# Wider score products, unread TensorE products at the ends of the passes, and a shorter direct ending in a two-layer decode kernel

## The chip, the cores and the metric

The kernel runs on one core of one Trainium2 chip. The metric is the device time of one execution in microseconds (us). A core has TensorE (matrix products, written to PSUM), VectorE (DVE), ScalarE (ACT), GpSimd (POOL) and SyncE (SP), which here issues nearly all loads from device memory. A product of 32-bit floats is two instructions on TensorE in the trace, so a count in a trace row is twice the count in a row of the program's order.

## The reference

Two layers with the same weights, each an attention over a cache and a gated feed-forward block, for a batch of 2 and one new token each:

```python
# B, Sq, D = 2, 1, 448;  H, Sk, Dh = 16, 4096, 256;  F = 1792
def _A_ref(x, k_cache, v_cache, wq, wo):
    q = (x @ wq).reshape(B, Sq, H, Dh).transpose(0, 2, 1, 3)
    scores = jnp.einsum("bhqd,bhkd->bhqk", q, k_cache) * (Dh ** -0.5)
    p = _softmax(scores, axis=-1)
    o = jnp.einsum("bhqk,bhkd->bhqd", p, v_cache)
    return o.transpose(0, 2, 1, 3).reshape(B, Sq, H * Dh) @ wo

def _B_ref(x, W_gate, W_up, W_down):
    gate = x @ W_gate
    gate = gate * (gate > 0)
    return (gate * (x @ W_up)) @ W_down

x = x + _A_ref(_layernorm(x), k_cache, v_cache, wq, wo)
x = x + _B_ref(_layernorm(x), W_gate, W_up, W_down)
x = x + _A_ref(_layernorm(x), k_cache, v_cache, wq, wo)
x = x + _B_ref(_layernorm(x), W_gate, W_up, W_down)
```

Everything is float32. The caches do not fit on the chip, so each layer reads them from device memory: 561.5 MB over the run.

## The kernel before

A **unit** is one head of one batch element, 32 a layer. Its k and its v are 4 MB each, in four **chunks** of 1 MB. All loaded data lies in one SBUF tile, `arena`, cut into 27 places of 1 MB: six blocks of four, and three single ones. `pending` lists every load of the program in order; `pump` issues the next ones on SP (L127) as far as places are free, and `release` frees a place behind the last product that reads it and calls `pump`. Most k and v are loaded as whole blocks of 4 MB, the last twelve chunks of a pass one by one. The first layer goes through the units forward, the second backward; 22 chunks and one head's weights stay in the arena from the one to the other (`KEPT`). So while the first layer's feed-forward block runs, only four places are free for its eleven pieces of weights, and the later pieces, and the second layer's loads, wait until its products free more.

`attention` holds the loop over units that sets TensorE's order, since every engine works through its own list in program order:

- `score`: the products of q and one chunk of k. The scores of four groups of keys go to PSUM rows 0, 32, 64 and 96 of `raw`, 256 columns wide, two products for the two halves of the head dimension (L308). One copy a chunk by DVE to `found_s` (L314).
- `score_turn`: four products a chunk with the identity as right operand put the scores on the partitions (L321).
- `softmax_max`, `softmax_exp`: maximum (DVE, POOL), exponential and sum (ACT, POOL).
- `weigh`: probabilities times v, a chunk at a time, into four strips of 32 PSUM rows of `po` (L358), 512 columns wide.
- `out_copy`, `out_add` (ACT L369, DVE L372) collect the unit's result in `row`; `out_turn` (L380) and `out_keep` turn it, and `project` (L399) multiplies it by the output weights of the head, for every second unit, into `acc`. They come one unit later, behind the next unit's scores and softmax.
- `query` (L283, L286): q of the next head.

Behind the last unit `ffn` runs: `absorb` (L236, L238, L226, L228, L246) adds the attention's output to x and turns it; `proj` multiplies by the gate's half and then the up half of the first weights (L447, four strips, 448 columns, 32 in a row as two calls); L468 and L470 make the hidden vector; L474 and L476 turn it; L517 multiplies by the 14 chunks of the down weights in four strips (`pd`). In the second layer only the first seven chunks take that way and are summed into `y` by `add_rows` (L250); the other seven go straight to `y`, two rows of `acc` in the fourth strip (L522). `y` is copied by DVE and ACT (L540, L541) and written out by SP (L542).

Of the kernel before, what the change touches and what calls it, by code (L numbers as in the profile page):

```python
# [25 lines left out]
G, E = 4, 2  # L26
QN = E * P
# [39 lines left out]
def two_layers(  # L67
# [112 lines left out]
    found_s = consts.tile([P, 2, QN], F32, name="found_s")  # L180
# [30 lines left out]
    po_all = ps_o.tile([P, 2, 2 * DH], F32, name="po")  # L211
    nc.vector.memset(po_all, 0.0)

    raw = ps_r.tile([P, 2, 2 * DH], F32, name="raw")
    nc.vector.memset(raw, 0.0)
# [5 lines left out]
    y = acc[SUMS : SUMS + B]  # L221

# [44 lines left out]
    def attention(order, after, begun):  # L267
# [35 lines left out]
        def score(u, c):  # L303
            kt = get("k", order[u], c).rearrange("p (j g n) -> p j g n", j=2, g=G)
            half, at = c % 2, c // 2 * QN
            for j in range(2):
                for g in range(G):
                    nc.tensor.matmul(  # L308
                        raw[32 * g : 32 * g + 1, half, at : at + QN],
                        q_of[u][:, j, :], kt[:, j, g, :], start=(j == 0), stop=(j == 1),  # L310
                    )
# [4 lines left out]
        def score_turn(u, c):  # L316
            if c == 0:
                s_of[u] = ps_s.tile([P, NT], F32, name="small")
            for e in range(E):
                n = c * CT + e * G  # L320
                nc.tensor.matmul(  # L321
                    s_of[u][:, n : n + G], found_s[:, c % 2, e * P : (e + 1) * P], pick,
# [27 lines left out]
        def weigh(u, c):  # L350
# [3 lines left out]
            if c == 0:  # L354
                po_of[u] = po_all[:, u % 2]
# [9 lines left out]
            if ("v", order[u], c) not in after:  # L365
                release("v", order[u], c)

# [23 lines left out]
        def project(u):  # L391
# [4 lines left out]
            for c in range(2):  # L396
# [5 lines left out]
                )  # L402
            if ("h", h, 0) not in after:
# [31 lines left out]
    def ffn(last):  # L435
# [5 lines left out]
        def proj(half, parts):  # L441

            p = raw[:, half, :D]
            for n, (part, c, done) in enumerate(parts):
# [9 lines left out]
                if done:  # L454
                    release("in", "", part)
            return p
# [13 lines left out]
        nc.vector.tensor_mul(hid, pu, hid)  # L470

# [123 lines left out]
```

## Time and profile before

| What | Value |
|---|---|
| median of 3 runs | 1348.59 us (1343.89 to 1349.69) |
| the profiled execution | 1346.37 us, its span 1344.6 us |
| mean granted TensorE clock | 0.74 of full speed |
| busy TensorE / its weight loads | 1077.4 us (80%) / 476.1 us (35%) |
| busy DVE / ACT / POOL | 203.3 us (15%) / 93.4 us (7%) / 47.7 us (4%) |
| read from device memory | 561.52 MB, 418 GB/s over the span |
| chain that ended last | PE 65%, DMA 15%, unknown queue 14%, DVE 3%, issue 2%, ACT 1% |

The page cuts the span in 40 slices of 33.6 us. A timeline row gives start, duration, engine, line, operation, what it writes and reads, how many instructions were merged and, in brackets, how long the engine had been idle and what ended that. A row of a table of stages gives the stretch, its length, the busy time of TensorE, its weight loads, DVE, ACT and POOL with their counts, the granted clock, the share of the DMA engines' time, and GB/s. A row of SP gives the issue of a load; the view of the DMA issues gives the time from there until the data has landed.

### The profile page before, as it was taken

The numbers are of one execution on the slowest core, as the hardware profiler recorded it, in microseconds if no ns is written. First come the engines' busy times: TensorE is split into PE (matmuls) and PEld (weight loads), VectorE is DVE, ScalarE is ACT, GpSimd is POOL, SyncE is SP. The second block draws the span as 40 slices with busy tenths as digits, with TensorE's granted clock in tenths as the row PEclk, the third lists the DMA queues.
The fourth block names the chain that finished last, engine by engine and source line by source line (L and its number), as shares of the span: only waits on it lengthen the run. The fifth ranks groups of instructions, "written<-read, shape, count | busy, mean of one in ns | idle before, by whom it ended". The sixth has DMA issues, their size and how long they took to land.

```text
span 1344.6 us, 18672 instructions
## 1 busy us (share of the span) xinstructions
PE 1077.4 (80%) x8328; PEld 476.1 (35%) x8328; DVE 203.3 (15%) x676; ACT 93.4 (7%) x284; POOL 47.7 (4%) x134
## 2 busy tenths in 40 slices
PE   4887889787787787887878988678786788767977
PEld 2434234332332333343334433234242333333432
DVE  1111111111111111111112211111111111111111
ACT  1000000000000000000010000000000000000001
POOL 0000000000000000000000000000000000000000
PEclk9867776667767776766778896876776777677678
DMA  9999999999999999999969999999999999999996
GB/s 398 432 431 431 428 428 432 431 427 428 430 433 432 429 429 427 431 432 421 403 255 400 436 428 431 431 427 431 429 429 434 428 429 429 429 434 429 426 418 252
DMA packets 29607, 562.71 MB, mean 419 GB/s; under 512 B 3284, under 2 KB 3416, under 8 KB 10200
## 3 DMA queue, kind: packets, MB, share of 16 engines
q1 hardware_dynamic: 29524, 561.53, 98.0%
q8 instruction: 65, 1.06, 0.3%
q14 instruction: 14, 0.11, 0.0%
q10 hardware_dynamic: 4, 0.00, 0.0%
HBM read 561.52 MB, written 0.00 MB: 418 GB/s over the span
## 4 chain that ended last, share of the span: by engine, by line
PE 65%; DMA 15%; another core or an unknown queue 14%; DVE 3%; issue 2%; ACT 1%; SPq 0%; POOL 0%; POOLq 0%; DVEq 0%; ACTq 0%
PE raw L308 22%; PE po L358 20%; PE small L321 11%; DMA arena<-in_k_cache_dram 11%; PE pq L283 4%; DMA arena<-in_w_head_dram 4%; PE small L380 2%; PE acc L399 2%; DVE found_s L314 2%; PE pq L286 1%; PE raw L447 1%; DMA arena<-in_w_in_dram 1%; PE raw L517 0%; PE acc L522 0%
## 5 line engine op out<-in xcount | busy, mean ns | idle before, releaser
L308 PE MATMUL raw<-arena,q 128*1 128x256 f32 x4096 | 360.2, 481 | 176.3 <-DMA arena<-in_k_cache_dram 140.0
L358 PE MATMUL po<-arena,probs 128*2 128x512 f32 x2048 | 343.9, 812 | 48.0 <-DMA arena<-in_v_cache_dram 43.1
L308 PEld LDWEIGHTS raw<-arena,q 128*1 128x1 f32 x4096 | 91.9, 91 | 376.3 <-issue 147.1
L321 PEld LDWEIGHTS small<-ident,found_s 128*128 128x128 f32 x1024 | 176.2, 248 | 123.1 <-issue 118.8
L321 PE MATMUL small<-ident,found_s 128*128 128x4 f32 x1024 | 196.2, 301 | 0.3
L314 DVE COPY found_s<-raw 128x256 f32<-128x256 f32 x256 | 108.6, 424 | 475.1 <-PE raw L308 474.6
L358 PEld LDWEIGHTS po<-arena,probs 128*2 128x2 f32 x2048 | 63.7, 103 | 293.3 <-issue 271.8
L372 DVE SCALAR_TENSOR_TENSOR row<-po,ri,row 128x256 f32<-128x256 f32 x64 | 31.0, 484 | 379.8 <-ACT row L369 379.8
L283 PE MATMUL pq<-xs,arena 128*128 128x2 f32 x384 | 71.6, 303 | 0.4 <-DVE xs L246 0.4
L283 PEld LDWEIGHTS pq<-xs,arena 128*128 128x128 f32 x384 | 68.9, 263 | 1.9 <-DVE total L256 1.5
L335 ACT ACTIVATE nm<-top,nsr 128x1 f32<-128x1 f32 x64 | 18.8, 294 | 726.2 <-POOL top L330 726.2
L330 POOL PARTITION_ALL_REDUCE top<-mx x64 | 22.5, 351 | 1184.7 <-DVE mx L328 1152.3
L369 ACT ACTIVATE row<-po,ri 128x256 f32<-128x256 f32 x64 | 30.3, 473 | 446.1 <-PE po L358 446.1
L399 PE MATMUL acc<-arena,oT 128*2 128x448 f32 x128 | 45.5, 804 | 8.1 <-DVE oT L389 8.1
L380 PE MATMUL small<-ones,row 128*128 128x1 f32 x256 | 48.5, 294 | 2.2 <-DVE row L372 2.2
L380 PEld LDWEIGHTS small<-ones,row 128*128 128x128 f32 x256 | 45.8, 252 | 4.9 <-DVE row L372 4.9
L286 PE MATMUL pq<-xs,arena 128*128 128x2 f32 x128 | 30.4, 307 | 0.0
L286 PEld LDWEIGHTS pq<-xs,arena 128*128 128x128 f32 x128 | 28.0, 270 | 0.0
L342 POOL PARTITION_ALL_REDUCE total<-rs x64 | 24.5, 383 | 63.5 <-ACT probs L338 63.5
L338 ACT ACTIVATE probs<-small,nm,sr 128x32 f32<-128x32 f32 x64 | 24.1, 377 | 2.1
L328 DVE TENSOR_REDUCE mx<-small 128x1 f32<-128x32 f32 x64 | 12.3, 191 | 62.9 <-PE small L321 62.9
L447 PE MATMUL raw<-arena,xs 128*32 128x448 f32 x128 | 16.6, 661 | 5.4 <-DMA arena<-in_w_in_dram 3.1
(90 smaller groups left out, 134.9 us busy)
## 6 DMA issues: line engine op xcount, KB each, us to landing
arena<-in_k_cache_dram SPq DMA_DIRECT2D x57, 4096.0 KB, 54.0
arena<-in_v_cache_dram SPq DMA_DIRECT2D x56, 4096.0 KB, 54.0
arena<-in_w_head_dram SPq DMA_DIRECT2D x31, 896.0 KB, 48.8
arena<-in_v_cache_dram SPq DMA_DIRECT2D x22, 1024.0 KB, 19.8
arena<-in_k_cache_dram SPq DMA_DIRECT2D x16, 1024.0 KB, 19.8
arena<-in_w_in_dram SPq DMA_DIRECT2D x14, 896.0 KB, 18.9
arena<-in_w_out_dram SPq DMA_DIRECT2D x4, 896.0 KB, 12.0
arena<-in_w_out_dram SPq DMA_DIRECT2D x3, 672.0 KB, 7.8
```

Source lines behind the costliest of these rows:

```text
L283: nc.tensor.matmul(pq[:, j, :], w[:, at : at + P], xT[:, c, :], start=(c == 0), stop=False)
L286: nc.tensor.matmul(pq[:, j, :], w[:, FULL * DH : FULL * DH + P], xT[:, FULL + j, :], start=False, stop=True,)
L308: nc.tensor.matmul(raw[32 * g : 32 * g + 1, half, at : at + QN], q_of[u][:, j, :], kt[:, j, g, :], start=(j == 0), stop=(j == 1),)
L314: nc.vector.tensor_copy(found_s[:, half, :], raw[:, half, at : at + QN])
L321: nc.tensor.matmul(s_of[u][:, n : n + G], found_s[:, c % 2, e * P : (e + 1) * P], pick, start=True, stop=True,)
L342: nc.gpsimd.partition_all_reduce(r_of[u], rs, P, RED.add)
L358: nc.tensor.matmul(po_of[u][32 * t : 32 * t + 2, :], p_of[u][:, n : n + 2], vt[:, 2 * t * DH : (2 * t + 2) * DH], start=(c == 0), stop=(c ...
L369: nc.scalar.activation(row[:, :DH], po_of[u][:, :DH], AF.Copy, scale=r_of[u][:, 0:1])
L372: nc.vector.scalar_tensor_tensor(row[:, :DH], po_of.pop(u)[:, DH:], r_of[u][:, 1:2], row[:, :DH], op0=ALU.mult, op1=ALU.add,)
L380: nc.tensor.matmul(pT_of[u][:, c : c + 1], row[:, c * P : (c + 1) * P], ones, start=True, stop=True,)
L399: nc.tensor.matmul(acc[at : at + B], oT_of[h][:, c, :], wo[:, c * D : (c + 1) * D], start=(n < 3), stop=(n >= n_u - 3),)
L447: nc.tensor.matmul(p[32 * j : 32 * j + 32, :], xs[:, c, :], w[:, j * D : (j + 1) * D], start=(n == 0), stop=(n == 3),)
```

## The change

Four things are changed.

1. **Scores.** A chunk of k now holds one half of the head dimension for 2048 keys (the host lays it out that way), and `score` makes four products of 512 columns a chunk instead of eight of 256. Two chunks fill one PSUM bank (`raw[0]`, `raw[1]`), and one copy of 512 columns takes a bank to `found_s`, the other to `row`. The turns of a unit come in two groups of eight products. `out_turn` and `out_keep` of the unit before move between the second and third chunk, `project` between the two groups of turns.
2. **Unread products.** `busy(n, half)` issues n products of the identity with a 512-column view of the identity into rows 0 and 1 of a bank of `po` that nobody reads then. It stands behind each chunk of `score` in a pass's last unit, behind each chunk of `weigh` in its last two, behind the last `project`, behind three of the four chunks of the second half of `proj`, around the turning of the hidden vector, between the chunks of the down weights, and in the first layer before `absorb`. All of it is left out of the output.
3. **Ending.** In the second layer eleven chunks of the down weights go through `pd`, and the last three straight to `y`, so `near` holds three products instead of fourteen. `y` is copied in one piece by ACT.
4. **PSUM.** `po` and `raw` are two tiles of one bank each instead of one tile of two.

```diff
-G, E = 4, 2
-QN = E * P
+G, E = 4, 4
...
+    def busy(n, half):
+
+        for _ in range(n):
+            nc.tensor.matmul(
+                po_all[half][:B], ident[:, :B],
+                ident[:, None, :].to_broadcast([P, 4, P]), start=True, stop=True,
+            )
...
-            kt = get("k", order[u], c).rearrange("p (j g n) -> p j g n", j=2, g=G)
-            half, at = c % 2, c // 2 * QN
-            for j in range(2):
-                for g in range(G):
-                    nc.tensor.matmul(
-                        raw[32 * g : 32 * g + 1, half, at : at + QN],
-                        q_of[u][:, j, :], kt[:, j, g, :], start=(j == 0), stop=(j == 1),
-                    )
+            kt = get("k", order[u], c).rearrange("p (g n) -> p g n", g=G)
+            half, j = c // 2, c % 2
+            for g in range(G):
+                nc.tensor.matmul(
+                    raw[half][32 * g : 32 * g + 1, :], q_of[u][:, j, :], kt[:, g, :],
+                    start=(j == 0), stop=(j == 1),
+                )
             if ("k", order[u], c) not in after:
                 release("k", order[u], c)
-            nc.vector.tensor_copy(found_s[:, half, :], raw[:, half, at : at + QN])
+            if u >= n_u - 1:
+                busy(2, u % 2)
+
+        def score_copy(u, half):
+            nc.vector.tensor_copy(row if half else found_s, raw[half])
...
             if ("v", order[u], c) not in after:
                 release("v", order[u], c)
+            if u >= n_u - 2:
+                busy(2, (u + 1) % 2)
...
+            if u == n_u - 1:
+                busy(1, 0)
             if ("h", h, 0) not in after:
                 release("h", h, 0)
...
             if_pair(score, u, 0)
-            for c in range(1, NC):
-                if_pair(score, u, c)
-                if_pair(score_turn, u, c - 1)
-            if_pair(score_turn, u, NC - 1)
+            if_pair(score, u, 1)
+            if_pair(score_copy, u, 0)
+            if_pair(out_turn, u - 1)
+            if_pair(out_keep, u - 1)
+            if_pair(score, u, 2)
+            if_pair(score, u, 3)
+            if_pair(score_copy, u, 1)
+            if_pair(score_turn, u, 0)
+            if_pair(project, u - 1)
+            if_pair(score_turn, u, 1)
             if_pair(softmax_max, u)
             if_pair(softmax_exp, u)
-            if_pair(out_turn, u - 1)
-            if_pair(out_keep, u - 1)
-            if_pair(project, u - 1)
...
                 if done:
                     release("in", "", part)
+                if half and n < 3:
+                    busy(2, 0)
...
         nc.vector.tensor_mul(hid, pu, hid)
+        busy(1, 0)
...
+        busy(2, 0)
         hT = row[:, : FULL * P].rearrange("p (m r) -> p m r", m=FULL)
...
-        n_pd = 7 if last else 14
+        n_pd = 11 if last else 14
...
-                    nc.tensor.matmul(y, close[k], w_k, start=False, stop=(k == 13))
+                    nc.tensor.matmul(y, near[:, k - n_pd], w_k, start=False, stop=(k == 13))
...
             release("out", "", j)
+            if j < 3:
+                busy(2, 0)
         if not last:
+            busy(1, 0)
             absorb(pd, P, scaled, nscaled)
...
-    nc.vector.tensor_copy(found[:, : D // 2], y[:, : D // 2])
-    nc.scalar.activation(found[:, D // 2 :], y[:, D // 2 :], AF.Copy)
+    nc.scalar.activation(found, y, AF.Copy)
```

How the order of TensorE moves at the last unit of the second pass (unit 31, counted from 0). Before, from the end of unit 30's `weigh` to the softmax of unit 31, L380 being `out_turn` of unit 30:

```order
L358 MATMUL po<-arena,probs 2x512 x16
L308 MATMUL raw<-arena,q 1x256 x16
L321 MATMUL small<-ident,found_s 128x4 x2
L308 MATMUL raw<-arena,q 1x256 x8
L321 MATMUL small<-ident,found_s 128x4 x2
L308 MATMUL raw<-arena,q 1x256 x8
L321 MATMUL small<-ident,found_s 128x4 x4
L380 MATMUL small<-ones,row 128x1 x2
```

In the changed kernel the same stretch, from the last chunk of unit 30's `weigh` (L368 now; L313 is `score`, L331 `score_turn`, L392 `out_turn`, L224 `busy`):

```order
L368 MATMUL poa<-arena,probs 2x512 x4
L224 MATMUL pob<-ident 2x512 x2
L313 MATMUL rawa<-arena,q 1x512 x4
L224 MATMUL pob<-ident 2x512 x2
L313 MATMUL rawa<-arena,q 1x512 x4
L224 MATMUL pob<-ident 2x512 x2
L392 MATMUL small<-ones,row 128x1 x2
L313 MATMUL rawb<-arena,q 1x512 x4
L224 MATMUL pob<-ident 2x512 x2
L313 MATMUL rawb<-arena,q 1x512 x4
L224 MATMUL pob<-ident 2x512 x2
L331 MATMUL small<-ident,found_s 128x4 x4
```

The turns went from between the chunks to behind all four, and two unread products stand behind every chunk.

At the end of the program TensorE before had, from the second half of `proj` (L447) to the last product (L474 and L476 turn the hidden vector):

```order
L447 MATMUL raw<-arena,xs 32x448 x16
L474 MATMUL raw<-ident,row 128x128 x3
L476 MATMUL raw<-ident,row 64x128 x2
L517 MATMUL raw<-arena,row 32x448 x7
L250 MATMUL acc<-row,scaled 2x448
L522 MATMUL acc<-arena,row 2x448 x7
```

In the changed kernel, from the turning (L494, L496) on, with the down chunks in L533 and the direct ones in L538:

```order
L494 MATMUL rawa<-ident,row 128x128 x3
L496 MATMUL rawa<-ident,row 64x128 x2
L224 MATMUL poa<-ident 2x512 x2
L533 MATMUL rawb<-arena,row 32x448 x4
L224 MATMUL poa<-ident 2x512 x2
L533 MATMUL rawb<-arena,row 32x448 x3
L224 MATMUL poa<-ident 2x512 x2
L533 MATMUL rawb<-arena,row 32x448 x4
L256 MATMUL acc<-row,scaled 2x448
L224 MATMUL poa<-ident 2x512 x2
L538 MATMUL acc<-arena,row 2x448 x3
```

Four chunks moved from the direct products to those in four strips, and each piece of the down weights but the last has two unread products behind it. The order of SP's loads is the same in both kernels.

More of the change, by code (lines that the diff above doesn't have):

```diff
@@ L209, in two_layers @@
     rstd = consts.tile([P, B], F32, name="rstd")
[L211 to L215, printed above, removed]
+    po_all = [ps_o.tile([P, 2 * DH], F32, name=f"po{k}") for k in "ab"]
+    raw = [ps_r.tile([P, 2 * DH], F32, name=f"raw{k}") for k in "ab"]
+    for bank in (*po_all, *raw):
+        nc.vector.memset(bank, 0.0)
     pick = ident.rearrange("p (g r) -> p g r", r=32)[:, :, 0]
@@ L441, in proj @@
         def proj(half, parts):
-            p = raw[:, half, :D]
+            p = raw[half][:, :D]
             for n, (part, c, done) in enumerate(parts):
@@ L470, in ffn @@
         nc.vector.tensor_mul(hid, pu, hid)
-        ph = raw[:, 0, :].rearrange("p (m r) -> p m r", m=4)
+        busy(1, 0)
+        ph = raw[0].rearrange("p (m r) -> p m r", m=4)
         for m in range(FULL):
@@ L495, in ffn @@
             nc.vector.tensor_mul(square, rstd, rstd)
[L496 removed]
+            near = row[:, D : D + 3 * B].rearrange("p (k b) -> p k b", k=3)
+            last_full = hT[:, 2, 96:].rearrange("p (b r) -> p b r", b=B)[..., 0]
+            nc.vector.tensor_mul(near[:, 0], last_full, square)
             nc.vector.tensor_mul(
[L498 to L503 removed]
+                near[:, 1:], tails.rearrange("p m (b r) -> p m b r", b=B)[..., 0],
                 square[:, None, :].to_broadcast([P, 2, B]),
             )
[L506 to L509 removed]
+        pd = raw[1][:, :D]
+        n_pd = 11 if last else 14
         for j in range(4):
```

25 lines of the change are left out of this document (8 added, 17 removed).

## The prediction

> **What bounds the kernel now.** I read the page first (the slices and the DMA queue), then a table of stages, then the timeline at the two pass ends.
>
> ```profile
> span 1344.6 us, 18672 instructions
> PEclk9867776667767776766778896876776777677678
> GB/s 398 432 431 431 428 428 432 431 427 428 430 433 432 429 429 427 431 432 421 403 255 400 436 428 431 431 427 431 429 429 434 428 429 429 429 434 429 426 418 252
> q1 hardware_dynamic: 29524, 561.53, 98.0%
> ```
>
> The loads run at about 430 GB/s in nearly every slice. Only the slice in the middle (255) and the last one (252) fall short. TensorE has a clock of 0.6 to 0.8 in most slices, and that costs nothing there. The table of stages says how much is at stake: core time, busy times by engine, granted clock, DMA share, GB/s.
>
> ```profile
> 33.60:654.00 620.40, 506.90 (x3864) 225.01 (x3856) 90.85 (x292) 38.31 (x124) 22.78 (x62) 0.71 1.00 429
> 669.00:708.00 39.00, 29.07 (x191) 13.41 (x191) 7.04 (x32) 5.86 (x13) 0.00 (x0) 0.78 0.65 246
> 708.00:1327.00 619.00, 499.43 (x4033) 219.67 (x4036) 95.12 (x313) 42.15 (x133) 23.48 (x64) 0.75 1.01 429
> 1327.00:1344.60 17.60, 11.96 (x69) 3.07 (x69) 2.05 (x7) 1.33 (x4) 0.00 (x0) 0.99 0.25 101
> ```
>
> Between the pass ends the DMA share is 1.00: whatever TensorE does there is hidden. At 669 to 708 us the queue runs short, because the arena is full of kept chunks and the next loads wait for TensorE to get through the feed-forward block (39.00 us at 246 instead of 429 GB/s: about 16.6 us lost). After 1327 us nothing is left to load. So only the chain of TensorE from the end of a pass's attention to the next loads, or to the output, sets the time, and the forecast is how much that chain grows or shrinks, twice.
>
> **The price of an unread product.** Both kernels' long products can be read here; all rows are of the last pass end.
>
> ```profile
> 1289.20 1.23 PE L321 MATMUL small<-ident,found_s 128*128 128x4 f32 x8
> 1292.06 3.61 PE L358 MATMUL po<-arena,probs 128*2 128x512 f32 x32
> 1307.51 6.52 PE L358 MATMUL po<-arena,probs 128*2 128x512 f32 x32 [0.78 <-ACT probs L338]
> 1333.03 1.70 PE L517 MATMUL raw<-arena,row 128*32 128x448 f32 x14 [1.14 <-ACT row L485]
> 1335.39 0.91 PE L250 MATMUL acc<-row,scaled 128*2 128x448 f32 x2 [0.65 <-ACT row L524]
> 1336.14 5.42 PE L522 MATMUL acc<-arena,row 128*2 128x448 f32 x14
> 1323.60:1342.40 18.80, 14.57 (x89) 3.84 (x81) 2.49 (x9) 1.97 (x6) 0.00 (x0) 1.00 0.42 170
> ```
>
> L522 puts all its products into one 32-row strip of PSUM: 14 instructions one behind the other in 5.42 us, 0.376 us each for 448 columns once the last one's drain (0.16 us) is taken off. L358 spreads 32 over four strips: 8 in a row in 3.61 us, 0.43 us each for 512 columns (last drain 0.19). So strips run beside each other, and one strip takes one product after the other. Each product is two instructions. **busy(2)** is therefore four instructions of 512 columns, all into rows 0 and 1, the first strip: 4 x 0.43 = 1.72 us at full clock. busy(1) is 0.86. A chunk of a score or of L358 needs 2 instructions on each strip, 0.86 us, so a chunk with busy(2) behind it holds the first strip for 2.58 us.
>
> **Do the gaps hold them?** Rows of the last two units of the second pass:
>
> ```profile
> 1282.18 1.45 PE L308 MATMUL raw<-arena,q 128*1 128x256 f32 x16 [4.45 <-DMA arena<-in_k_cache_dram]
> 1299.57 1.76 PE L308 MATMUL raw<-arena,q 128*1 128x256 f32 x16 [0.86 <-DMA arena<-in_k_cache_dram]
> 1302.20 1.89 PE L308 MATMUL raw<-arena,q 128*1 128x256 f32 x16
> 1311.89 0.10 PEld L358 LDWEIGHTS po<-arena,probs 128*2 128x2 f32 x4 [0.86 <-DMA arena<-in_v_cache_dram]
> 1316.01 0.92 PE L399 MATMUL acc<-arena,oT 128*2 128x448 f32 x4 [0.25 <-DVE oT L389]
> 1320.20 4.90 PE L447 MATMUL raw<-arena,xs 128*32 128x448 f32 x32 [0.36 <-DVE xs L246]
> 1326.94 3.21 PE L447 MATMUL raw<-arena,xs 128*32 128x448 f32 x32 [0.78 <-ACT row L468]
> 1342.10 0.35 ACT L541 ACTIVATE row<-acc 2x224 f32<-2x224 f32 x1 [6.76 <-DVE row L540]
> 1299.80:1313.40 13.60, 12.82 (x76) 5.25 (x72) 1.59 (x6) 0.76 (x3) 0.73 (x2) 0.50 1.01 419
> ```
>
> Unit 30's scores start when its k lands (1282.18, hard bound). Its L358 at 1292.06 does not wait for data: 3.61 us without a pause. From its end (1295.67) to the third chunk of unit 31's scores (1299.57) TensorE has 3.9 us, of which two scores of about 1.05 and a turn of 0.6 (half of L321's 1.23) take 2.7. That is the room. Into it go four busy(2) of weigh(30) and two of score(31), 10.3 us. So the unread products push the chain behind the data, and once it is behind no later gap is left for them; each one then costs its 1.72 us.
>
> **Tail, step by step** (time in the trace of before; lead of the changed kernel over it). Scores of unit 30 as 512-column products and both copies first, then all turns: the last turn ends later, as the turns (8 instructions, 1.23 us) no longer lie under the next copy, and project stands between them: weigh(30) at 1292.9, +0.8. Four chunks of 2.58: first strip free at 1303.2. Scores of unit 31, 4 x 2.58 and out_turn's 0.55: 1314.0. Two turns of 1.1 and the softmax (1.63 from L321's end at 1290.43 to 1292.06): 1317.9. weigh(31): 3 x 2.58 + 0.86 + 0.19 = 8.8, and 1.2 for the granted clock, which I expect to fall for one stretch as the turns stream four columns: 1327.9, against 1314.03 before, +13.9. The last busy(2) delays out_turn by about 0.5: project at 1330.3, +14.3. From there to L447 before took 4.19 at half clock; I take 3.2: 1333.6, +13.4. First half of the gate 3.2 instead of 4.90 and its tail: second half at 1338.5, +11.6. There three busy(2) stand between four chunks that all have landed: 3.21 + 5.16: 1346.9, against 1330.15, +16.7. busy(1) and busy(2) around the transposes: the first lies under the multiply, the second overhangs by 0.4: +17.1. Down: before 1333.03 to 1342.45, 9.42. Now 11 chunks in three rounds of 0.75 with two busy(2) between (5.85 with the drain), copy 0.6, sum 0.75, three chunks on one strip 2.4, one copy 0.55: 10.2. **Tail +17.5** (four serial chunks and a copy less are worth 3.2; the two busy(2) take 3.4).
>
> **Middle.** The same chain, with its loads:
>
> ```profile
> 637.04 1.04 PE L308 MATMUL raw<-arena,q 128*1 128x256 f32 x16 [0.80 <-DMA arena<-in_k_cache_dram]
> 645.64 4.94 PE L358 MATMUL po<-arena,probs 128*2 128x512 f32 x32
> 670.86 0.92 PE L399 MATMUL acc<-arena,oT 128*2 128x448 f32 x4 [0.25 <-DVE oT L389]
> 675.05 4.91 PE L447 MATMUL raw<-arena,xs 128*32 128x448 f32 x32 [0.36 <-DVE xs L246]
> 676.83 2.78 SPq L127 DMA_DIRECT2D arena<-in_w_in_dram  x3
> 687.63 0.96 PE L447 MATMUL raw<-arena,xs 128*32 128x448 f32 x8 [1.23 <-DMA arena<-in_w_in_dram]
> 691.48 4.89 PE L517 MATMUL raw<-arena,row 128*32 128x448 f32 x28 [1.14 <-ACT row L485]
> 698.80 1.28 PE L283 MATMUL pq<-xs,arena 128*128 128x2 f32 x6 [0.36 <-DVE xs L246]
> 705.96 0.33 SPq L127 DMA_DIRECT2D arena<-in_k_cache_dram  x1
> ```
>
> weigh(30) at 645.7 as before; 10.3 and 1.1 at the lower clock: 657.1; scores 10.85: 668.0; turns and softmax 3.9: 671.9; weigh(31) 8.8 + 1.7: 682.4; project 684.3 (+13.4); L447 687.5 (+12.4); the first freed weight slot 0.9 later (before 1.8, from 675.05 to SP's 676.83), 688.4 (+11.6), so the loads stand still that much longer. The second half was bound by those loads (687.63) and is now bound by its own 8.3 from 692.4: 700.7; down starts at 703.9 (+12.4) and takes 4 x 0.75 + 3 x 1.72 + 0.16 = 8.3 instead of 4.89: 712.2. From there to the next k before took 9.6 (696.37 to 705.96), 2.4 of it up to the query; I take 2.6 for that and half of the rest at full clock, about 6 in all: the next k is issued at 718.1, **+12.1** against 705.96. All SP's later issues queue behind it, and the queue is full to 1327, so this shift reaches the end whole.
>
> What costs nothing: the score's new shape in the other 60 units. It halves the score's instructions and replaces four DVE copies of 256 columns by two of 512. A gain lies behind loads at 1.00, and a loss would have to exceed the idle 18% of TensorE first; bounds 0 and 0. `near`'s smaller products run on DVE beside L517.
>
> One term rests on whether the final y products wait behind the last busy(2). They go to the fourth strip, the unread ones to the first.
>
> ```profile
> 702.57 0.91 PE L250 MATMUL acc<-row,scaled 128*2 128x448 f32 x1
> 702.57 1.03 PE L308 MATMUL raw<-arena,q 128*1 128x256 f32 x6
> 703.27 0.95 PE L250 MATMUL acc<-row,scaled 128*2 128x448 f32 x1
> ```
>
> Both L250 stand ahead of L308 in the program, yet six L308 of other strips start before L250's second. So I let y pass for nothing; the bound is 1.3 to 1.7. [...]
>
> Sum: 1344.6 + 12.1 + 17.5 = 1374.2, and 1.8 around the span (the profiled execution took 1346.4): **1376**. The runs' median is 1348.6, 2 above the profiled one, inside the range.
>
> **Rivals.**
> (A) Faster: the unread products fit into waits, and the warm clock is the net effect. For it: half clock at 1299.80 to 1313.40, where L358 takes 6.52 against 3.61. The tail would then be bound by the loads:
>
> ```profile
> arena<-in_w_out_dram SPq DMA_DIRECT2D x1, 224.0 KB, 14.1
> 1320.65 0.33 SPq L127 DMA_DIRECT2D arena<-in_w_out_dram  x1
> ```
>
> last landing 1334.8, one product and copy 1.5: 1336.3, 6 sooner; in the middle L358 1, the sums 1, L447 1.5, the query 1.5, 5 sooner: 1335. It decides at the price: a busy(2) would have to cost under about 0.4 us, against 1.72 by L522 and L358. [...] 8%.
> (B) Nothing: gain and price cancel, 1342 to 1353, if half of the fillers meet waits. 5%.
> (C) The filler is too narrow to hold the clock, and everything runs at half: another 20 or so per end, 1400 to 1440. Against it: L522, as narrow, ran at 1.00 from 1323.60 to 1342.40. 4%.
> (D) Half-way, 1353 to 1361: 3%.
>
> **Numbers.** Forecast 80%: 1361 to 1390 holds two more or two fewer half-clock stretches per end (1.7 each) and the y wait of 1.7. Within 0.5% (about what a measurement of this kernel can tell from no change) 5%, faster 8%, slower 87%.
>
> **To be seen.** L358 of unit 30 spread over about 10 us with unread products of 0.43 each; no DMA wait in unit 31's scores; DMA share 0 for some 12 us longer near 680 to 718; three rounds of 2.5 in the gate's second half. Wrong if unit 31's chunks still wait for DMA behind their fillers, or if the fillers' starts lie much closer than 0.43.

## The result, and the profile after

The changed kernel takes 1383.22 us (median of 4 runs, 1380.48 to 1383.80) against 1348.95 us for the kernel before in the same session: a ratio of 1.026, with a 95% interval of 1.0239 to 1.0282. It is 34.3 us slower. The forecast was 1376 us, in a range of 1361 to 1390. The profiled execution took 1383.27 us, 2.0 of it around the span.

The page of the changed kernel, from its parts on the span, the slices, the DMA queue, the chain of waits and the groups (L224 is `busy`):

```profile
span 1381.3 us, 14695 instructions
PEclk9878666677687767766998887777666667888899
GB/s 400 437 428 429 433 427 426 434 431 430 432 429 427 435 428 433 428 431 418 181 235 406 432 436 425 436 428 428 433 430 427 434 430 430 431 427 429 423 419 32
q1 hardware_dynamic: 29524, 561.53, 95.3%
PE 72%; another core or an unknown queue 15%; DMA 7%; issue 2%; ACT 2%; POOL 1%; DVE 1%; POOLq 0%; ACTq 0%
L224 PE MATMUL poa<-ident 128*2 128x512 f32 x98 | 48.1, 610 | 0.0
```

The loads stream as before in all slices but those at the two pass ends, which are worse: 181 and 235 in the middle, where one slice stood at 255 before, and 32 in the last, against 252. The same bytes now take 95.3% of the DMA engines' time over the span instead of 98.0%. DMA's part of the chain fell from 15% to 7% and TensorE's rose from 65% to 72%. The row of L224 counts the unread instructions in one bank of `po`; 64 more stand in the other. The clock stands at 0.8 to 0.9 in the last five slices, where it was 0.6 to 0.8. TensorE runs faster there, and the kernel ends later.

The table of stages (columns as before) of both pass ends:

```profile
673.60:692.90 19.30, 17.06 (x99) 6.26 (x102) 2.80 (x14) 3.15 (x7) 0.73 (x2) 1.00 0.00 1
692.90:725.00 32.10, 31.73 (x177) 11.52 (x173) 3.98 (x19) 3.51 (x9) 0.00 (x0) 0.92 0.64 252
1352.20:1381.30 29.10, 25.27 (x140) 6.91 (x139) 3.12 (x14) 2.44 (x7) 0.00 (x0) 1.00 0.00 1
```

In the middle nothing at all is loaded for 19.3 us, with TensorE at full clock and busy for 17.06 of it. At the end the last load has landed 29.1 us before the span is over. The timeline of the middle, TensorE and SP's queue (start, duration; in brackets the idle time before and what ended it):

```profile
635.22 3.59 PE L313 MATMUL rawa<-arena,q 128*1 128x512 f32 x16 [3.48 <-DMA arena<-in_k_cache_dram]
650.09 1.89 PE L368 MATMUL poa<-arena,probs 128*2 128x512 f32 x8 [1.63 <-ACT probs L348]
...
657.09 1.45 PE L368 MATMUL poa<-arena,probs 128*2 128x512 f32 x5
658.38 1.45 PE L224 MATMUL pob<-ident 128*2 128x512 f32 x3
...
659.67 1.45 PE L368 MATMUL poa<-arena,probs 128*2 128x512 f32 x5
...
664.39 0.60 PE L313 MATMUL rawa<-arena,q 128*1 128x512 f32 x3
...
667.91 0.61 PE L392 MATMUL small<-ones,row 128*128 128x1 f32 x4
668.45 1.04 PE L313 MATMUL rawb<-arena,q 128*1 128x512 f32 x8
...
677.27 1.04 PE L368 MATMUL pob<-arena,probs 128*2 128x512 f32 x8 [1.63 <-ACT probs L348]
...
691.84 3.21 PE L464 MATMUL rawa<-arena,xs 128*32 128x448 f32 x32 [0.36 <-DVE xs L252]
692.86 1.83 SPq L126 DMA_DIRECT2D arena<-in_w_in_dram  x3
...
718.57 0.83 PE L289 MATMUL pq<-xs,arena 128*128 128x2 f32 x6 [0.36 <-DVE xs L252]
725.00 0.33 SPq L126 DMA_DIRECT2D arena<-in_k_cache_dram  x1
```

Chunks of `weigh` stand 2.58 us apart (657.09 to 659.67), three unread instructions take 1.45 with the last one's drain of 0.16, and from 650.09 to SP's 692.86 no product of TensorE waits for a load. From unit 30's first score to the next layer's first load of k it is 89.78 us (635.22 to 725.00), against 68.92 before (637.04 to 705.96): +20.9. The same view of the end:

```profile
1299.63 3.44 PE L313 MATMUL rawa<-arena,q 128*1 128x512 f32 x16 [4.60 <-DMA arena<-in_k_cache_dram]
1309.99 1.86 PE L368 MATMUL poa<-arena,probs 128*2 128x512 f32 x8 [1.63 <-ACT probs L348]
...
1336.58 1.15 PE L368 MATMUL pob<-arena,probs 128*2 128x512 f32 x8 [1.63 <-ACT probs L348]
...
1375.33 0.54 PE L256 MATMUL acc<-row,scaled 128*2 128x448 f32 x1 [0.67 <-ACT row L540]
1375.33 0.59 PE L224 MATMUL poa<-ident 128*2 128x512 f32 x1
1376.08 0.54 PE L538 MATMUL acc<-arena,row 128*2 128x448 f32 x1
1376.19 0.59 PE L224 MATMUL poa<-ident 128*2 128x512 f32 x1
...
1379.15 0.33 SPq L560 DMA_DIRECT2D out_dram<-row  x1
```

From unit 30's first score to the output's issue it is 79.52 us against 60.29 (1282.18 to 1342.47): +19.2. Unit 30's scores start 1.8 us earlier in the first pass than before, and from the first k issue of the second pass to unit 30's scores 574.6 us pass instead of 576.2. So the span's +36.7 is 20.9 + 19.2 - 1.8 - 1.6.

### The profile page after: what moved, and what is told of

It is laid out like the page before. It is cut to its first block, busy times and chain, and to the rows that moved or that the text cites. A ratio compares the mean times of both kernels' runs of the same rounds, so it can differ in the third digit from the quotient of the medians.

```text
span 1381.3 us, 14695 instructions
## 1 busy us (share of the span) xinstructions
PE 1066.5 (77%) x6442; PEld 387.3 (28%) x6442; DVE 183.7 (13%) x549; ACT 93.6 (7%) x284; POOL 47.7 (3%) x134
## 3 DMA queue, kind: packets, MB, share of 16 engines
q1 hardware_dynamic: 29524, 561.53, 95.3%
## 4 chain that ended last, share of the span: by engine, by line
PE 72%; another core or an unknown queue 15%; DMA 7%; issue 2%; ACT 2%; POOL 1%; DVE 1%; POOLq 0%; ACTq 0%
PE pob L368 12%; PE poa L368 12%; PE rawa L313 11%; PE rawb L313 10%; PE small L331 10%; DMA arena<-in_k_cache_dram 3%; DMA arena<-in_v_cache_dram 3%; PE small L392 3%; PE pq L289 3%; PE poa L224 3%; PE acc L411 3%; PE pob L224 2%; ACT probs L348 1%; PE pq L292 1%
## 5 line engine op out<-in xcount | busy, mean ns | idle before, releaser
L313 PE MATMUL rawa<-arena,q 128*1 128x512 f32 x1024 | 174.7, 794 | 151.1 <-DMA arena<-in_k_cache_dram 151.1
L368 PE MATMUL pob<-arena,probs 128*2 128x512 f32 x1024 | 185.3, 863 | 90.3 <-DMA arena<-in_v_cache_dram 87.0
L368 PE MATMUL poa<-arena,probs 128*2 128x512 f32 x1024 | 180.5, 842 | 52.8 <-ACT probs L348 52.8
L313 PE MATMUL rawb<-arena,q 128*1 128x512 f32 x1024 | 162.2, 750 | 0.0
L313 PEld LDWEIGHTS rawa<-arena,q 128*1 128x1 f32 x1024 | 25.7, 92 | 265.4 <-issue 205.1
L331 PEld LDWEIGHTS small<-ident,found_s 128*128 128x128 f32 x512 | 74.4, 223 | 73.9 <-issue 70.4
L368 PEld LDWEIGHTS pob<-arena,probs 128*2 128x2 f32 x1024 | 30.7, 107 | 210.7 <-issue 206.2
L331 PEld LDWEIGHTS small<-ident,row 128*128 128x128 f32 x512 | 72.7, 219 | 32.3 <-issue 32.3
L331 PE MATMUL small<-ident,found_s 128*128 128x4 f32 x512 | 79.9, 279 | 0.0
L331 PE MATMUL small<-ident,row 128*128 128x4 f32 x512 | 77.4, 274 | 0.0
L368 PEld LDWEIGHTS poa<-arena,probs 128*2 128x2 f32 x1024 | 29.4, 105 | 168.1 <-issue 112.5
L392 PEld LDWEIGHTS small<-ones,row 128*128 128x128 f32 x256 | 44.2, 245 | 82.1 <-issue 63.1
L289 PE MATMUL pq<-xs,arena 128*128 128x2 f32 x384 | 53.7, 256 | 0.4 <-DVE xs L252 0.4
L289 PEld LDWEIGHTS pq<-xs,arena 128*128 128x128 f32 x384 | 49.9, 198 | 1.9 <-DVE total L262 1.5
L392 PE MATMUL small<-ones,row 128*128 128x1 f32 x256 | 49.7, 298 | 0.0
L224 PE MATMUL poa<-ident 128*2 128x512 f32 x98 | 48.1, 610 | 0.0
L313 PEld LDWEIGHTS rawb<-arena,q 128*1 128x1 f32 x1024 | 22.7, 90 | 62.1 <-issue 60.9
```

The source lines that it names most:

```text
L224: nc.tensor.matmul(po_all[half][:B], ident[:, :B], ident[:, None, :].to_broadcast([P, 4, P]), start=True, stop=True,)
L289: nc.tensor.matmul(pq[:, j, :], w[:, at : at + P], xT[:, c, :], start=(c == 0), stop=False)
L313: nc.tensor.matmul(raw[half][32 * g : 32 * g + 1, :], q_of[u][:, j, :], kt[:, g, :], start=(j == 0), stop=(j == 1),)
L331: nc.tensor.matmul(s_of[u][:, n : n + G], rows[:, e * P : (e + 1) * P], pick, start=True, stop=True,)
L368: nc.tensor.matmul(po_of[u][32 * t : 32 * t + 2, :], p_of[u][:, n : n + 2], vt[:, 2 * t * DH : (2 * t + 2) * DH], start=(c == 0), stop=(c ...
L392: nc.tensor.matmul(pT_of[u][:, c : c + 1], row[:, c * P : (c + 1) * P], ones, start=True, stop=True,)
```

## Experiments

Eleven kernels. "Mid" is the profiled time from unit 30's first score to the next layer's first load of k, "tail" from unit 30's first score in the second pass to the output's issue. "To before" is the median's difference from the kernel before on the same chip, so rows of different sessions may be compared by it. Unread instructions are counted as the trace counts them, two a product.

| Kernel | unread | mid | tail | median | to before | ratio (95%) |
|---|---|---|---|---|---|---|
| before | 0 | 68.92 | 60.29 | 1348.95 | | |
| after | 162 | 89.78 | 79.52 | 1383.22 | +34.3 | 1.026 (1.0239 to 1.0282) |
| e1_no_unread | 0 | 68.14 | 58.05 | 1339.62 | -8.0 | 0.9941 (0.9922 to 0.9959) |
| e2_unread_on_before | 162 | 83.50 | 84.82 | 1388.68 | +41.1 | 1.0291 (1.0244 to 1.0338) |
| e3_ending_only | 0 | 67.85 | 58.78 | 1346.17 | -1.5 | 0.9994 (0.9983 to 1.0005) |
| e4_two_strips | 162 | 75.77 | 65.42 | 1353.76 | +6.1 | 1.0038 (1.0022 to 1.0055) |
| e5_attention_only | 100 | 80.95 | 67.82 | 1365.86 | +17.5 | 1.0139 (1.0095 to 1.0183) |
| e6_feed_forward_only | 62 | 70.61 | 65.41 | 1350.01 | +1.7 | 1.0017 (1.0006 to 1.0028) |
| e7_only_in_idle | 44 | 64.79 | 56.43 | 1335.54 | -12.8 | 0.9901 (0.9886 to 0.9916) |
| e8_quarter_length | 162 | 71.72 | 62.90 | 1345.69 | -2.6 | 0.9976 (0.9956 to 0.9995) |
| e9_warm_unit30 | 170 | 86.94 | 83.44 | 1375.74 | +28.4 | 1.0221 (1.0183 to 1.0258) |
| e10_twice_as_many | 324 | 121.31 | 113.06 | 1449.09 | +101.7 | 1.075 (1.0725 to 1.0776) |
| e11_idle_more | 58 | 63.36 | 56.51 | 1334.31 | -13.1 | 0.9901 (0.9883 to 0.9918) |

**Is it the unread products?** The first removes them and keeps the rest of the change:

```diff
-        for _ in range(n):
+        for _ in range(0):
```

> The changed kernel without its unread products; all that is read is computed. Theory (the unread products displace the chain at both pass ends, and nothing else of the change costs): the chain falls back to about that of before, less the shorter ending (about 2.5 us): span 1336 to 1346, 35 to 45 us under the changed kernel, and in the profile unit 31's last two score chunks wait for DMA again. Rival (the new order of scores and turns, or the half clock at unit 30's scores that it brings, is what costs): 1360 to 1380.

It is 8.0 us faster than the kernel before, so the unread products cost 42.3 us (34.3 + 8.0). The waits they had covered are back, in its timeline:

```profile
655.05 1.04 PE L313 MATMUL rawb<-arena,q 128*1 128x512 f32 x8 [1.01 <-DMA arena<-in_k_cache_dram]
664.99 1.04 PE L368 MATMUL pob<-arena,probs 128*2 128x512 f32 x8 [1.21 <-DMA arena<-in_v_cache_dram]
...
1293.16 5.69 PE L368 MATMUL poa<-arena,probs 128*2 128x512 f32 x32 [1.63 <-ACT probs L348]
...
1317.96 4.84 PE L464 MATMUL rawa<-arena,xs 128*32 128x448 f32 x32 [0.35 <-DVE xs L252]
```

Unit 31's products wait for their loads by about 1 us at a time, and unit 30's `weigh` and the gate run at a low clock, 5.69 and 4.84 us (at 1.00 the kernel before took 3.61 for its `weigh`, the changed kernel 3.21 for this half of the gate). The waits and the slow gate are what the unread products did away with (in unit 30's `weigh` the clock still stood at 0.53 from 1309.99 to 1313.60 in the changed kernel), and that was worth less than their price. The opposite run puts them into the kernel before, at the same places (the first of them shown):

```diff
+    def busy(n, half):
+        for _ in range(n):
+            nc.tensor.matmul(
+                po_all[:B, half], ident[:, :B],
+                ident[:, None, :].to_broadcast([P, 4, P]), start=True, stop=True,
+            )
...
             nc.vector.tensor_copy(found_s[:, half, :], raw[:, half, at : at + QN])
+            if u >= n_u - 1:
+                busy(2, u % 2)
...
```

> The kernel before with the unread products at the same places, nothing else of the change. Theory: 28 to 42 us over the kernel before, 1376 to 1391, with chunks of unit 31 about 2.6 us apart and no wait for DMA between them. Rival (it is the new order of scores): 1345 to 1355.

+41.1 us (its four executions lie 29.9 to 43.8 above). The price is that of the unread products, in either order of the scores.

**The ending by itself**, on the kernel before (`near` shortened and `y` copied in one piece, as in the change):

```diff
...
-        n_pd = 7 if last else 14
+        n_pd = 11 if last else 14
...
-    nc.vector.tensor_copy(found[:, : D // 2], y[:, : D // 2])
-    nc.scalar.activation(found[:, D // 2 :], y[:, D // 2 :], AF.Copy)
+    nc.scalar.activation(found, y, AF.Copy)
```

> The kernel before with the new ending alone (eleven down chunks in four strips, three straight to y, one copy). Theory: four serial chunks of 0.75 become one round of 0.75 and one copy of 0.55 stands for two of 0.8, so 2.5 us under the kernel before: 1344 to 1348. Rival (the ending waits for its last loads, or the copies overlap anyway): within 1 us of before.

Its timeline:

```profile
1333.21 2.46 PE L512 MATMUL raw<-arena,row 128*32 128x448 f32 x22 [1.14 <-ACT row L485]
1336.32 0.91 PE L250 MATMUL acc<-row,scaled 128*2 128x448 f32 x2 [0.65 <-ACT row L519]
1337.07 2.42 PE L517 MATMUL acc<-arena,row 128*2 128x448 f32 x6
```

The output is issued at 1340.15, 6.94 us behind the first of these rows, where the kernel before needed 9.44 (1333.03 to 1342.47): 2.5 us saved in that stretch. The runs give 1.5 us, in an interval that holds no change. What is left of the change without unread products is 6.6 us more (e1 against e3, same chip): the scores' new order and width and the PSUM tiles together; no run takes these apart.

**How much does one cost, and what in it?** Twice as many; a quarter of the columns; and the two products of a pair on two strips (their copies were in the first strip both):

```diff
-        for _ in range(n):
+        for _ in range(2 * n):
```

> The changed kernel with twice as many unread products at every place. Theory (no gap is left, so each further one costs its full streaming time): some 20 busy(2) more in the middle and 19 at the end, 1.72 each, 60 to 70 us: 1443 to 1455. Rival (a part of them still lies in waits): 1400 to 1435.

```diff
-                po_all[half][:B], ident[:, :B],
-                ident[:, None, :].to_broadcast([P, 4, P]), start=True, stop=True,
+                po_all[half][:B, :P], ident[:, :B], ident, start=True, stop=True,
```

> The changed kernel with unread products of 128 instead of 512 columns, as many, at the same places. Theory (the price is streaming time on the first strip): a busy(2) costs 0.43, a chunk with one 1.29 us, and most of them fit: 1340 to 1348. Rival (a price per instruction, 0.2 or more each whatever the length): 1355 to 1370.

```diff
-        for _ in range(n):
+        for s in range(n):
             nc.tensor.matmul(
-                po_all[half][:B], ident[:, :B],
+                po_all[half][32 * s : 32 * s + B], ident[:, :B],
```

> The changed kernel with the two products of a busy(2) in the first and the second strip of 32 PSUM rows instead of both in the first; as many unread instructions of the same size. Theory (one strip takes its products one after the other, and the first strip is the slowest): a busy(2) costs 0.86 instead of 1.72, so chunks are 1.72 us apart, and about 12 us go at each pass end: 1353 to 1364. Rival (each unread instruction has its price wherever it goes, by issue order or by weight load): 1380 to 1386, as the changed kernel.

Doubling adds 67.4 us for 162 more instructions, 0.42 us each: nearly the full streaming time of 0.43, since hardly a wait is left to hold them. The first 162 cost 42.3 us, 0.26 each; by the price of the second set they would be 67.4, so an estimate from these two is that waits and the faster clock gave back about 25. With a quarter of the columns and the same number of instructions, 5.4 us are left over e1: the price goes with the columns streamed, not with the instructions. On two strips 14.1 are left. Its timeline shows why:

```profile
655.28 0.59 PE L224 MATMUL pob<-ident 128*2 128x512 f32 x2
655.29 1.44 PE L368 MATMUL poa<-arena,probs 128*2 128x512 f32 x6
...
657.01 1.44 PE L368 MATMUL poa<-arena,probs 128*2 128x512 f32 x6
```

The chunks stand 1.72 us apart (655.29 to 657.01) instead of 2.58: the two unread products of a pair run beside each other, and one less of them stands in the first strip's line.

**Which places?** One half of them each, with `busy` left out of `ffn` in the first, and of `score`, `weigh` and `project` in the second:

```diff
-                if half and n < 3:
-                    busy(2, 0)
...
-        busy(1, 0)
...
-        busy(2, 0)
...
```

> The changed kernel with the unread products of the attention alone (behind scores, weigh and the last project); those of the feed-forward block are left out. Theory: in the last block three busy(2) of the up half (5.2), two between the down chunks (3.4) and the overhang behind the turning (0.8) go, 9.5 us; in the first block 5 to 8 us, since its up half then waits for its loads: 1364 to 1370. Rival (the feed-forward ones lie in waits and are free): 1380 to 1386.

```diff
-            if u >= n_u - 1:
-                busy(2, u % 2)
...
-            if u >= n_u - 2:
-                busy(2, (u + 1) % 2)
...
-            if u == n_u - 1:
-                busy(1, 0)
```

> The changed kernel with the unread products of the feed-forward block alone; those of the attention are left out. Theory: the same 9.5 us at the end and 0 to 5 in the middle over the kernel without any: 1349 to 1354. Rival (they are free, or the clock they hold pays for them): 1336 to 1341.

Over e1 the attention's cost 25.5 us (17.5 + 8.0) and the feed-forward block's 9.7; both together cost 42.3, 7.1 more than the sum. The feed-forward part by itself still finds waits to fill in the middle (mid 70.61 against 68.14 in e1), and at the end it pays, where nothing is waited for: from the gate's first product to the output's issue it takes 27.91 us (1318.07 to 1345.98) against 18.38 in e1 (1317.96 to 1336.34), 9.5 us more, as expected. The tails differ by less, 65.41 against 58.05, as unit 30's scores took another time in the two: 8.71 us to `weigh` here, 14.87 in e1. Its timeline at the end, in the gate's second half:

```profile
1324.66 1.45 PE L224 MATMUL poa<-ident 128*2 128x512 f32 x3
...
1327.13 1.45 PE L224 MATMUL poa<-ident 128*2 128x512 f32 x3
...
1329.60 1.45 PE L224 MATMUL poa<-ident 128*2 128x512 f32 x3
```

Rounds of 2.47 us: a chunk of 0.75 and two unread products of 0.86.

**Does the idea work where TensorE really waits?** The unread products taken from between the chunks of the attention and put where the timeline of e1 shows TensorE idle: ahead of unit 30's scores, behind the softmax of the last two units and ahead of the last `out_turn`; in the feed-forward block one instead of two, none between products in the second layer, and none ahead of the first layer's `absorb`.

```diff
...
         for u in range(n_u + 1):
+            if u == n_u - 2:
+                busy(2, u % 2)
+            if u == n_u:
+                busy(1, u % 2)
...
                 query(u + 1)
+            if n_u - 2 <= u < n_u:
+                busy(1, u % 2)
...
-                if half and n < 3:
-                    busy(2, 0)
+                if half and n < 3 and not last:
+                    busy(1, 0)
...
-        busy(2, 0)
+        busy(1, 0)
...
-            if j < 3:
-                busy(2, 0)
+            if j < 3 and not last:
+                busy(1, 0)
...
```

> The changed kernel with unread products only where the run without any showed TensorE idle: two ahead of unit 30's scores (2.1 and 3.7 us idle), one in the softmax of units 30 and 31 (1.63 idle), one ahead of the last out_turn (1.1 idle), one behind the last project, one on each side of the turning, and in the first block one behind pieces that wait for loads. Theory: none displaces anything and the clock stays up: 3 us less in the middle and 3 at the end (bound by the last load) than the run without any: 1331 to 1338. Rival (the granted clock does not follow, or the chain is bound by loads already): 1338 to 1342.

This kernel is faster than both: 0.9901, 12.8 us (one per cent) under the kernel before and 4.8 under e1. Its timeline and its stage (lines behind the edit have shifted, L366 is `weigh`, L466 the gate, L535 the down products):

```profile
635.41 1.90 PE L313 MATMUL rawa<-arena,q 128*1 128x512 f32 x16 [2.23 <-DMA arena<-in_k_cache_dram]
644.12 3.61 PE L366 MATMUL poa<-arena,probs 128*2 128x512 f32 x32 [0.68 <-ACT probs L346]
655.16 1.04 PE L313 MATMUL rawb<-arena,q 128*1 128x512 f32 x8 [1.44 <-DMA arena<-in_k_cache_dram]
...
1319.80 0.96 PE L466 MATMUL rawb<-arena,xs 128*32 128x448 f32 x8 [1.23 <-DMA arena<-in_w_in_dram]
1325.78 0.96 PE L535 MATMUL rawb<-arena,row 128*32 128x448 f32 x8 [0.83 <-DMA arena<-in_w_out_dram]
```

```profile
634.30:657.40 23.10, 17.52 (x138) 6.24 (x138) 3.97 (x10) 1.24 (x4) 0.73 (x2) 1.00 1.01 420
```

The same eight score products take 1.90 us, at a granted clock of 1.00, where after's take 3.59, at 0.50; `weigh` takes 3.61 at both ends where e1's takes 5.20 and 5.69, and up to the very last down chunk TensorE waits for loads (0.83 us there): the data is the bound again. A step further, one unread product behind three of the last unit's score chunks and one ahead of the first layer's `absorb`:

```diff
+            if u == n_u - 1 and c < 3:
+                busy(1, u % 2)
...
```

> The run with unread products only in idle time, and one more behind each of unit 31's first three score chunks (0.9 to 1.45 us idle there) and one ahead of the first layer's absorb (0.8 idle). Theory: nothing displaced, the clock stays up for the softmax side of unit 31 and the next query: 0 to 2.5 us less, 1333 to 1336. Rival (the last chunks find TensorE late): 1336.5 to 1340.

1334.31 us (1333.48 to 1335.12) against e7's 1335.54 (1335.1 to 1335.9), on another chip: not told apart from it by the ratios, 0.9901 both. In the tail unit 30's first eight score products took 3.18 us in e7 and 1.90 in e11, and the tails are 56.43 and 56.51: where the data is the bound, as there, the faster scores were worth nothing. In the timeline of e11 the query at the end of the first layer is not slowed: its first six instructions on L289 take 0.83 us and the next six 0.81, where after's take 0.83 and 1.34 and the granted clock falls to 0.50 at 719.60.

```profile
693.80 0.83 PE L289 MATMUL pq<-xs,arena 128*128 128x2 f32 x6 [0.36 <-DVE xs L252]
...
694.72 0.81 PE L289 MATMUL pq<-xs,arena 128*128 128x2 f32 x6
```

The next k is issued at 698.68, 4.9 us behind the first of these rows, where the changed kernel needs 6.43 from there and the kernel before 7.16.

**The low clock in unit 30's scores.** The changed kernel plus two unread products ahead of unit 30's scores:

```diff
         for u in range(n_u + 1):
+            if u == n_u - 2:
+                busy(2, u % 2)
             if_pair(score, u, 0)
```

> The changed kernel with one busy(2) more in each pass, ahead of unit 30's scores, where TensorE waits for the load of k. Theory (the 9 us that the middle grew beyond the forecast are unit 30's scores at half clock, 6, and the next query at half clock, 3): the clock is up for unit 30's scores, the stretch from the landing of unit 30's k to the next layer's first issue of k falls from 89.9 to 83 to 86, the time by 4 to 8: 1375 to 1380. Rival (those 9 us are unread products that cost more than their streaming): stretch 89 to 92, time 1382 to 1386.

```profile
630.83 1.88 PE L224 MATMUL poa<-ident 128*2 128x512 f32 x4
635.40 3.06 PE L313 MATMUL rawa<-arena,q 128*1 128x512 f32 x16 [2.70 <-DMA arena<-in_k_cache_dram]
639.34 3.59 PE L313 MATMUL rawb<-arena,q 128*1 128x512 f32 x16
```

The median fell to 28.4 us over the kernel before (from 34.3). But the profiled execution is the slowest of the four (1384.53; the others 1373.85 to 1377.35), and in it the second half of the scores takes 3.59 us all the same. That holding the clock there brings the 5.9 us is not shown; the run is inconclusive on the cause.

## Why the prediction was right, and which terms were off

The mechanism is the one that was predicted: an unread product takes its whole streaming time in the first strip (0.42 us an instruction in e10; with a quarter of the columns 5.4 of the 42.3 us are left in e8, on two strips 14.1 in e4), the chain falls behind the loads within unit 30's `weigh`, and from there on no wait for a load is left to hide the next one. The signs named beforehand appear: chunks 2.58 us apart, no wait for data in unit 31's scores, no load at all from 673.6 to 692.9, and rounds of 2.5 us in the gate's second half (unread products at 1357.84, 1360.31 and 1362.77). Step by step, in us, the middle from unit 30's first score to the next k, the tail to the output's issue:

| Step | mid predicted | mid measured | tail predicted | tail measured |
|---|---|---|---|---|
| first score of unit 30 to its `weigh` | 8.7 | 14.9 | 10.7 | 10.4 |
| `weigh` of unit 30 | 11.4 | 11.7 | 10.3 | 11.1 |
| scores of unit 31, `out_turn` | 10.9 | 11.9 | 10.8 | 11.9 |
| turns and softmax | 3.9 | 3.6 | 3.9 | 3.6 |
| `weigh` of unit 31, to `project` | 12.4 | 11.2 | 12.4 | 12.9 |
| `project` to the gate | 3.2 | 3.3 | 3.3 | 3.3 |
| gate's first half | 4.9 | 4.2 | 4.9 | 4.2 |
| second half and hidden vector | 11.5 | 10.9 | 21.4 with down, output | 22.1 |
| down | 8.3 | 9.2 | | |
| to the next k | 5.9 | 8.9 | | |
| sum | 81.1 | 89.8 | 77.7 | 79.5 |

The sum came out 7.1 us short: 8.7 in the middle, 1.8 at the tail, and 3.4 the other way outside the pass ends. Three terms make up 5.8 of it: +6.2, +3.0 and -3.4.

**"weigh(30) at 645.7 as before"** is the largest: 14.9 us instead of 8.7, so +6.2. After's table of stages, cut where the granted clock changes, has the reason:

```profile
630.80:634.20 3.40, 0.94 (x9) 0.00 (x0) 0.48 (x1) 0.47 (x1) 0.00 (x0) 1.00 0.90 381
634.20:654.70 20.50, 17.86 (x74) 6.15 (x75) 2.12 (x6) 0.76 (x3) 0.73 (x2) 0.50 1.01 420
654.70:719.60 64.90, 62.30 (x328) 18.77 (x324) 8.14 (x33) 5.39 (x14) 0.73 (x2) 1.00 0.56 226
719.60:726.40 6.80, 6.80 (x35) 3.41 (x38) 0.67 (x4) 1.75 (x3) 0.00 (x0) 0.50 0.21 61
```

All of unit 30's scores and turns ran at 0.50. The prediction carried the 8.60 us of one execution of the kernel before over to another program. Up to this `weigh`, after, e1, e4, e5, e6, e8 and e10 are one and the same program, and their profiles show how far the stretch swings. The first rows of unit 30's scores in e1, e5 and e6, from their timelines:

```profile
635.27 3.54 PE L313 MATMUL rawa<-arena,q 128*1 128x512 f32 x16 [2.14 <-DMA arena<-in_k_cache_dram]
...
635.07 1.90 PE L313 MATMUL rawa<-arena,q 128*1 128x512 f32 x16 [0.97 <-DMA arena<-in_k_cache_dram]
...
635.15 3.52 PE L313 MATMUL rawa<-arena,q 128*1 128x512 f32 x16 [4.63 <-DMA arena<-in_k_cache_dram]
```

From there to `weigh` it took 8.71 us behind a wait of 0.97 (e5), 10.35 behind 2.14 (e1), 14.87 behind 3.47 to 3.51 (after, e4, e8) and 10.36 behind 4.60 and 4.63 (e10, e6). In the order of the kernel before, the wait was 0 to 0.80 and the stretch 8.60 to 8.64 in all three first passes that were profiled (before, e2, e3). So in the new order TensorE mostly waits longer for this k, and the stretch can run at the low clock, 0.50 in after. One and the same program came out at all of these values, so the 14.87 of after's profiled execution is one draw of several, and the forecast had no term for that. The first 16 instructions took 1.90 us behind the wait of 0.97 (e5) and 3.59 and 3.52 behind 3.48 and 4.63 (after, e6), but also 3.54 behind 2.14 (e1) and 3.06 behind 2.70 (e9), while behind 2.13 in e6's tail the whole stretch took 8.71. Nor did the longest waits bring the slowest stretch, so the length of the wait by itself does not settle it. In the tail the same term was right within 0.3, behind a wait of 4.60 us: the first scores took 3.44 us, the next ones 1.90.

**"Half of the rest at full clock, about 6 in all"**: 8.9 us from the end of the down products (716.14) to the next k, +3.0. Up to the query it took 2.43 us, where 2.6 was allowed; the rest took 6.43, where about 3.4 was left. The clock fell again at 719.6, to 0.50, in a stretch in which TensorE is busy for 6.80 of 6.80 us.

**What costs nothing** was a term with the wrong size, on the other side: the new order and width of the scores, with the PSUM tiles, are worth about 6.6 us by the medians (e1 against e3), where the bounds were 0 and 0. The profiles of e1 and e3 differ by 3.8, since e3's is its fastest execution; of that 1.9 lies ahead of unit 30 in the first pass (635.27 against 637.13) and 1.5 between the pass ends (574.9 against 576.4). Loads stand at a share of 1.00 there in both, so the price was not where the argument looked for it. What in the loads runs ahead was not found out.

That the total stayed within its range owes something to luck. The forecast charged the unread products about 32 us (29.6, and the 2.6 that the ending was to save), where after against e1 shows 42.3, and it gave nothing for the 6.6 us that go the other way.

The smaller terms add up to 1.3 us. `out_turn` cost 1.5 us instead of 0.55 at both ends: its products take all four strips (128 rows of `small`), so the third chunk of unit 31's scores began at 668.45, where 2.57 behind the second's 664.39 would be 666.96. The stretch of half clock expected in the middle's `weigh` of unit 31 did not come, though the same turns of four columns stood ahead of it (the clock was 1.00 from 654.70 to 719.60), and in the tail one came in either unit's (0.53 from 1309.99 to 1313.60 and from 1338.00 to 1341.00); that such turns bring the clock down was the author's assumption, and the runs do not show it. That `y` passes the unread products held: L256 and L224 start in the same moment, 1375.33, and L538 starts between unread ones. The ending's own saving was 2.5 us in e3, against 2.6 by the terms of the prediction (10.2 less the two busy(2)' 3.4 is 6.8, against 9.42). The tail's sum holds a slip: +17.1 at the down products and 10.2 instead of 9.42 from there make +17.9, not +17.5.

Of the rivals, "faster" failed at the price it named: a pair would have to cost under 0.4 us, and doubling shows 1.7 for a pair (four instructions of 0.42). Where the products really stand in idle time, its time did come out: 1335 was its sum, and e7 measures 1335.54. That is in part luck: by the profiles the pass ends gave 8.0 us (4.1 and 3.9), where the rival had 11, and the other 3.3 of e7's 11.3 us lie outside them, where it had nothing. The rival's argument for the clock was the 0.50 from 1299.80 to 1313.40, and that stretch stands behind waits of 0.58 and 0.86 us; that a filler in waits as short as these would have held the clock was not shown. The rival that everything runs at half clock fell with the stage at 1.00 from 654.70 to 719.60.

## What to carry to other kernels

Work that is only meant to keep a clock up was paid for in full once the chain it stood in was the bound (e10: 0.42 us for each further instruction), however free the engine looks as a mean; so put it ahead of a wait that the trace shows, in an amount shorter than that wait, and not between products whose data is already there (e7: 12.8 us under the kernel before, where the changed kernel is 34.3 over it). Where several products run beside each other in strips, spread the filler over them or count the strip that it fills (14.1 us on two strips, 42.3 on one). And run the change without its headline part: here the rest of the change was worth 8 us, and the fillers hid it.

## What the runs showed of the hardware

The granted clock stood at 0.50 while TensorE was busy for all 6.80 us of a stretch (719.60 to 726.40) and for 17.86 of 20.50 us in another (634.20 to 654.70, behind 3.40 us at 1.00 in which it was busy for 0.94). It stood at 1.00 from 654.70 to 719.60, where unread products in two rows of one strip stand between the others. The same program of unit 30, from first score to `weigh`, took from 8.71 us (e5) to 14.87 (after, e4, e8): its first 16 score instructions took 1.90 us in e5, 3.54 in e1 and 3.59 in after, the second 16 1.90 in e1 and 3.59 in after. What sets the moments at which the clock changes, no run here shows. Four of the kernels with unread products between the chunks also scatter more from execution to execution: 1377.6 to 1391.4 in e2, 1362.5 to 1376.4 in e5, 1339.0 to 1349.7 in e8 and 1373.9 to 1384.5 in e9, against 1335.1 to 1335.9 in e7.
